# Two expert layers on one core: VectorE and GpSimd in written order, token operands on GpSimd, and a quarter of the weights converted a layer later

## The chip, the cores and the metric

The kernel is one launch on one core of a Trainium2 chip. The time is that of the device, in microseconds, and lower is better. Five engines work side by side, each through its own queue in order: TensorE (PE in the profile; PEld is its weight load), VectorE (DVE), ScalarE (ACT), GpSimd (POOL) and SyncE (SP), which here only issues DMAs.

## The reference, cut to what matters

```python
X = np.fft.rfft(x, axis=1)                       # x: 2 x 3008 x 256
Yr, Yi = ...                                     # X @ (w_r + i w_i) + bias, soft-shrunk by 0.01
y = np.fft.irfft(Y, n=3008, axis=1)              # 6016 tokens of 256
h = y @ w_in;  g = h * np.cos(h);  x = g @ w_out             # layer 1: 256 -> 2048 -> 256
h = x @ w_in2; g = h * np.clip(h + 3, 0, 6) / 6; x = g @ w_out2   # layer 2, the same shapes
```

The expert weights come as 64-bit floats. The kernel turns them into 32-bit floats itself, with integer operations on their bits ("conversion" below).

## The kernel before

Three parts follow each other: the Fourier part, expert layer 1 and expert layer 2. Every product of an expert layer keeps 32-bit precision by splitting each operand into a rounded high part and the rest (low part) and adding three matmuls: high by high, high by low, low by high (`three`).

An expert layer has six stages of 1024 tokens (the last 896), each as two halves of 512 (448). A stage (`jj`) has eight steps (`STEPS`), so the two layers have 96 steps `k`; a step is step `q = k % 8` of its stage. In a step, seven products of sums of the four quarter matrices (a Strassen form) make four blocks of h in four PSUM banks, called ha, hb, hc, hd: 21 matmuls. The four blocks of the step before (`Block`: ba, bd, be, bc) then go through w_out into `acc`: 24 matmuls. PE's order over the step is ha, (acc), hc, hb, ha, acc, hb, hd, acc, hb, acc.

Around it, each step has this work:
- ACT copies ha into hb (line 874) and hc into p5 (line 883). DVE then adds: `add(d, p5, b)` makes hd and `add(c, p5, b)` makes hc (line 764). PE can write hb again only when DVE has read it, so PE's next hb matmul waits for each add.
- For each block, `first` (ACT, then DVE) and, in layer 1 only, `second` (ACT Sin, DVE multiply, line 737) make g in the tile `r`; `split` rounds it to `gh` on ACT (line 743) and subtracts to get `gl` on POOL (line 744, through the helper at line 159).
- `operands(jj + 1)` makes the next stage's token operands `tok` out of the staged tokens `st`: four differences in place (`st<-st`) and seven subtractions for low parts (`tok<-st,tok`). Here DVE does them (line 399), but for four low parts in layer 1, which POOL does. It is a generator; `advance` takes one of its five pieces at a time, from the fifth step of a stage on. ACT writes the high parts.
- The `Converter` turns weights from 64 to 32 bits in chunks (kind "i" for w_in, "o" for w_out; layer m, quarter c, half k): a magnitude on ACT, five operations on DVE (clamp, shift, top, exponent, rest: lines 189 to 201), an addition on POOL (line 162), for "i" four sums on POOL, then the split into high and low parts (`pieces`, ACT line 260 and POOL). `other` asks for one conversion step at two places of a step, three in the first half of a stage, where one more is taken at the end. Quarters 0 and 3 of layer 1 are split directly into their tiles in SBUF; all others go to DRAM and are loaded later (`load_wi`, `load_wo`). All of layer 2's weights are converted during layer 1.
- In the first 13 steps, `y_mm` and `y_out` also finish the last rows of the inverse transform (yp, yo).

The order on PE, ACT and SP is the order of the program text (`manual_schedule`). On DVE and POOL a scheduler at build time decides the order.

Of the kernel before, what the change touches and what calls it, by code (L numbers as in the profile page):

```python
# [122 lines left out]
def fourier_moe_moe_kernel(ctx, tc, x, w_r, w_i, b_r, b_i, ta, tg, fg, win1, wout1, win2, wout2, out):  # L123
# [42 lines left out]
    def convert(kind, m, c, k):  # L166
# [54 lines left out]
        def pieces():  # L221
            direct = m == 0 and c in (0, 3)
# [10 lines left out]
            def tile(z):  # L233
                return persist.tile([128, 2, 256], F32R, tag="whi", bufs=3, name=f"whi{name}{z}")
# [31 lines left out]
    class Converter:  # L266


        def __init__(self):
            self.queue, self.loaded = [], []  # L270
            self.finished = set()
            self.prev, self.begun = None, False
            self.course = iter(())

        def add(self, m):
            for c in range(4):
                self.queue += [("i", m, c, 0), ("i", m, c, 1), ("o", m, c, 0), ("o", m, c, 1)]
            while len(self.loaded) < 2:
                self.load()
# [14 lines left out]
        def chunk(self):  # L294
            tail = self.tail()
            if self.loaded:
                key, ops = self.loaded.pop(0)
                if not self.begun:
# [12 lines left out]
                if ops["split"]:  # L311
                    self.prev = (key, ops)
                self.load()
            else:
                yield from tail
# [67 lines left out]
    def operands(jj):  # L383
# [25 lines left out]
        halve(B22, st[:, 1, 1])  # L409
        sub(st[:, 0, 0], st[:, 0, 1], st[:, 0, 0])  # L410
        yield
        sub(st[:, 0, 1], st[:, 1, 1], st[:, 0, 1])
        sub(st[:, 1, 1], st[:, 1, 1], st[:, 0, 0])
        act.activation(at(hi, T1, 2), st[:, 0], AF.Copy)
        yield
        sub(st[:, 1, 0], st[:, 1, 0], st[:, 1, 1])
        halve(T1, st[:, 0, 0])
        halve(T3, st[:, 0, 1])
        act.activation(at(hi, T4, 2), st[:, 1], AF.Copy)
        yield  # L420
        halve(T4, st[:, 1, 0])
        halve(T2, st[:, 1, 1])


    with ExitStack() as actx:
        apool = actx.enter_context(tc.tile_pool(name="apool", bufs=1))
        with tc.manual_schedule(engines={mybir.EngineType.PE, mybir.EngineType.SP, mybir.EngineType.Activation}):
# [83 lines left out]
            def late_loads3():  # L511
                cv.add(0)
# [76 lines left out]
            def shrink_hi(b, p):  # L589
                sh = persist.tile([128, 2, D], F32R, tag="gh", bufs=5, name=f"sh{b}_{p}")  # L590
# [91 lines left out]
            for i in range(NB * NP):  # L682
# [15 lines left out]
                elif i > 19:  # L698
                    next(ready, None)
            next(ready, None)  # L700
# [6 lines left out]
    with tc.manual_schedule(engines={mybir.EngineType.PE, mybir.EngineType.SP, mybir.EngineType.Activation}):  # L707
# [4 lines left out]
        class Block:  # L712
# [65 lines left out]
        def finish(jj, t):  # L778
            m, p = divmod(jj, NJ)
            n = HALF[p]  # L780
            for d, a in enumerate(acc.pop((jj, t))):
                o = persist.tile([128, 512], F32, tag="o", bufs=3, name=f"o{jj}_{t}{d}")
                if m == 0:
                    act.activation(o[:, :n], a[:, :n], AF.Copy)
                    sp.dma_start(x_dram[1][p][d, :, t * n : (t + 1) * n], o[:, :n])
                else:
                    act.activation(o[:, :n], a[:, :n], AF.Copy, scale=1.0 / 6.0)
# [10 lines left out]
        def w_loads(k):  # L798

            if k < 4:  # L800
                c = k // 2 + 1
                if k % 2 == 0:
                    load_wi(0, c)
                else:
                    load_wo(0, 2 * c)
                    load_wo(0, 2 * c + 1)
            elif k in (4, 5):
                cv.require(("i", 0, 3, 1) if k == 4 else ("o", 0, 3, 1))
            q = k - (G - STEPS)
            if 0 <= q < STEPS + 2 and q % 2 == 1:  # L810
                if q < STEPS:
                    load_wi(1, q // 2)
                if q > 2:
                    load_wo(1, q - 3)
                    load_wo(1, q - 2)
# [3 lines left out]
        def prepare(k):  # L819
# [4 lines left out]
            if q == 3:  # L824
# [3 lines left out]
        def advance(k):  # L828
            if k % STEPS > 3:
                next(ready, None)  # L830

        def other():
# [3 lines left out]
            if not pend:  # L836
                cv.step(1)
# [13 lines left out]
        cv.add(1)  # L851
# [10 lines left out]
        for k in range(2 * G):  # L862
# [16 lines left out]
            flush()  # L879
# [7 lines left out]
            add(d, p5, b, n)  # L887
            mm(a, A12, B21)
            prepare(k)
            advance(k)  # L890
            ba.first()
            flush()
# [3 lines left out]
            if k % STEPS < 4:  # L896
                other()
# [4 lines left out]
            other()  # L902
            bd.first()
            bc.first()
            out_next()
            y_begin()
            bd.second()
            y_end()
# [3 lines left out]
            advance(k)  # L912
# [3 lines left out]
            other()  # L916
            ba.split()
            old = bd, be, bc
            waiting += [ba, bd, be, bc]
            if k > 0 and k % STEPS < 4:  # L920
                cv.step(1)
# [51 lines left out]
```

## Time and profile before

| | before |
|---|---|
| median of 3 runs | 1261.34 us (1260.5 to 1261.72) |
| the profiled execution's own time | 1256.72 us |
| its span, first to last instruction | 1254.6 us |
| mean granted TensorE clock | 0.986 |
| PE busy | 1182.9 us (94%), 5377 matmuls |
| DVE busy | 814.6 us (65%), 1163 |
| ACT busy | 834.3 us (67%), 1530 |
| POOL busy | 680.8 us (54%), 536 |

The profile is of one execution. A group names the line, the engine and what is written from what. PE is busy nearly everywhere, so the shares say little; what counts is how long a step takes, and what PE waits for in a step that takes longer than another of its kind.

### The profile page before, as it was taken

Reading aid. Unit: us, or ns where it says so; the run is one execution under the profiler, and the core shown is the slowest. Engines: PE = TensorE matmul, PEld = TensorE weight load, DVE = VectorE, ACT = ScalarE, POOL = GpSimd, SP = SyncE. Lnnn points to the kernel's source line nnn. Section 1 sums busy time; section 2 is a strip of 40 time slices with the busy share of each in tenths; the row PEclk is TensorE's granted clock in tenths of the full one; section 3 lists DMA queues with packets and bytes.
Section 4 is the critical chain, followed back from the end, with each engine's and each line's share of the span. In section 5 each row is a group of like instructions: output and inputs, shape, how many; then the busy total and the mean of one; then the engine's idle time right before and its main releaser. Section 6 shows DMA issues by size and latency. Waiting matters only on the chain.

```text
span 1254.6 us, 15895 instructions
## 1 busy us (share of the span) xinstructions
PE 1182.9 (94%) x5377; PEld 975.7 (78%) x5379; DVE 814.6 (65%) x1163; ACT 834.3 (67%) x1530; POOL 680.8 (54%) x536
## 2 busy tenths in 40 slices
PE   8999979899988898989999999999999999999998
PEld 7888757687777676767778988788788887887897
DVE  4979695865586796896786684643744636436342
ACT  4677557677677777867777876556665566556654
POOL 0566335665466667676655554554545554555554
PEclk9999999999899899999999999999999999999999
DMA  9655837535410401320200435001010010010000
GB/s 249 186 153 147 268 96 223 182 96 161 158 66 17 160 34 43 118 85 34 102 21 1 179 132 189 1 1 68 1 60 8 1 68 1 1 63 1 34 1 30
DMA packets 51514, 107.75 MB, mean 86 GB/s; under 512 B 6404, under 2 KB 24328, under 8 KB 50664
## 3 DMA queue, kind: packets, MB, share of 16 engines
q1 hardware_dynamic: 51432, 106.74, 26.4%
q8 instruction: 42, 0.69, 0.2%
q14 instruction: 40, 0.33, 0.1%
HBM read 64.64 MB, written 42.07 MB: 85 GB/s over the span
## 4 chain that ended last, share of the span: by engine, by line
PE 65%; DVE 16%; ACT 6%; DMA 4%; issue 4%; POOL 3%; SPq 1%; POOLq 0%; ACTq 0%; DVEq 0%
PE acc L752 30%; PE hb L752 12%; PE ha L752 7%; PE hc L752 4%; PE hd L752 4%; DVE tok L399 3%; PE pp L537 3%; PE yp L355 2%; DVE r L737 2%; DVE r L728 2%; PE bp L564 2%; POOL gl L159 1%; DVE hc L764 1%; ACT gh L743 1%; PE zp L464 1%
## 5 line engine op out<-in xcount | busy, mean ns | idle before, releaser
L159 POOL TENSOR_TENSOR gl<-r,gh 128x512 fp32r<-128x512 f32 (+1 forms) x384 | 504.7, 1320 | 403.5 <-ACT gh L743 327.0
L752 PE MATMUL acc<-gh,wo 128*128 128x512 f32 (+1 forms) x1536 | 534.2, 389 | 0.0
L752 PEld LDWEIGHTS acc<-gh,wo 128*128 128x128 f32 x1536 | 291.3, 190 | 54.8
L752 PE MATMUL acc<-gl,wo 128*128 128x512 f32 (+1 forms) x768 | 299.3, 390 | 7.4 <-POOL gl L159 7.3
L752 PE MATMUL hb<-tok,wi 128*128 128x512 f32 (+1 forms) x864 | 247.8, 395 | 33.2 <-DVE hd L764 20.2
L743 ACT ACTIVATE gh<-r 128x512 fp32r<-128x512 f32 (+1 forms) x384 | 236.2, 616 | 9.8 <-DVE r L737 9.7
L752 PEld LDWEIGHTS hb<-tok,wi 128*128 128x128 f32 x864 | 160.4, 190 | 74.6 <-DVE hd L764 25.7
L752 PEld LDWEIGHTS acc<-gl,wo 128*128 128x128 f32 x768 | 145.7, 190 | 38.9 <-POOL gl L159 11.8
L752 PE MATMUL ha<-tok,wi 128*128 128x512 f32 (+1 forms) x576 | 160.6, 387 | 2.0 <-DMA wi<-wi_dram 1.2
L764 DVE TENSOR_TENSOR hd<-p,hb 128x512 f32<-128x512 f32 (+1 forms) x96 | 65.5, 683 | 144.7 <-PE hb L752 134.3
L736 ACT ACTIVATE r<-r 128x512 f32<-128x512 f32 (+1 forms) x192 | 118.8, 619 | 49.8 <-DVE r L728 49.4
L752 PEld LDWEIGHTS ha<-tok,wi 128*128 128x128 f32 x576 | 108.1, 188 | 23.3 <-ACT wi L260 1.6
L874 ACT ACTIVATE hb<-ha 128x512 f32<-128x512 f32 (+1 forms) x96 | 55.1, 574 | 52.0 <-PE ha L752 51.9
L883 ACT ACTIVATE p<-hc 128x512 f32<-128x512 f32 (+1 forms) x96 | 56.5, 589 | 49.8 <-PE hc L752 49.5
L764 DVE TENSOR_TENSOR hc<-p,hb 128x512 f32<-128x512 f32 (+1 forms) x96 | 65.3, 681 | 34.8 <-PE hb L752 34.6
L752 PE MATMUL hc<-tok,wi 128*128 128x512 f32 (+1 forms) x288 | 80.6, 388 | 5.3 <-DVE r L737 5.2
L752 PE MATMUL hd<-tok,wi 128*128 128x512 f32 (+1 forms) x288 | 82.4, 395 | 0.0
L737 DVE TENSOR_TENSOR r<-r,hb 128x512 f32<-128x512 f32 (+1 forms) x48 | 32.3, 673 | 63.3 <-ACT r L736 63.3
L730 ACT ACTIVATE r<-hd 128x512 f32<-128x512 f32 (+1 forms) x48 | 28.3, 589 | 62.4 <-PE hd L752 62.4
L752 PEld LDWEIGHTS hc<-tok,wi 128*128 128x128 f32 x288 | 53.5, 188 | 17.9 <-DVE r L737 8.2
L399 DVE TENSOR_TENSOR tok<-st,tok 128x512 fp32r<-128x512 f32 (+1 forms) x60 | 61.9, 1039 | 4.6 <-ACT tok L404 2.3
L752 PEld LDWEIGHTS hd<-tok,wi 128*128 128x128 f32 x288 | 55.7, 193 | 11.0
(140 smaller groups left out, 1684.3 us busy)
## 6 DMA issues: line engine op xcount, KB each, us to landing
wi<-wi_dram SPq DMA_DIRECT2D x6, 1792.0 KB, 7.5
st<-x_dram SPq DMA_DIRECT2D x20, 512.0 KB, 6.7
rawi<-in_win_dram SPq DMA_DIRECT2D x16, 512.0 KB, 4.6
rawo<-in_wout_dram SPq DMA_DIRECT2D x16, 512.0 KB, 3.9
u_dram<-v SPq DMA_DIRECT2D x48, 128.0 KB, 2.4
u_sb<-u_dram SPq DMA_DIRECT2D x16, 384.0 KB, 4.0
wo<-wo_dram SPq DMA_DIRECT2D x12, 512.0 KB, 8.2
x_dram<-o SPq DMA_DIRECT2D x20, 256.0 KB, 2.2
```

The costliest lines, as they stand in the source:

```text
L159: nc.gpsimd.tensor_tensor(out, x, y, op=ALU.subtract)
L355: pe.matmul(yp[:, i * TP : (i + 1) * TP], lhsT=u_sb[g][:, i, ec * 128 : (ec + 1) * 128], rhs=tg_sb[g][:, i * TP : (i + 1) * TP], start=Tru ...
L399: dve.tensor_tensor(out, x, y, op=ALU.subtract)
L537: pe.matmul(pp.rearrange("p a e -> p (a e)"), lhsT=za[:, p, kc, 2 * (k2 % 2) : 2 * (k2 % 2) + 2, :].rearrange("p r n -> p (r n)"), rhs=wb[ ...
L730: act.activation(r, h, AF.Relu, bias=3.0, scale=1.0)
L736: act.activation(r, r, AF.Sin, bias=math.pi / 2, scale=1.0)
L737: dve.tensor_tensor(r, r, self.h[:, : self.n], op=ALU.mult)
L743: act.activation(gh[:, :n], self.r[:, :n], AF.Copy)
L752: pe.matmul(h[:, :n], lhsT=w, rhs=x, start=start and j == 0, stop=stop and j == 2, skip_group_check=True)
L764: dve.tensor_tensor(h[:, :n], r[:, :n], x[:, :n], op=ALU.add)
L874: act.activation(b[:, :n], a[:, :n], AF.Copy)
L883: act.activation(p5[:, :n], c[:, :n], AF.Copy)
```

## The change

In the expert layers DVE and POOL join the engines that keep the order of the text. The token operands' eleven subtractions go to POOL, one at a time in twelve pieces (DVE keeps them for one stage, `jj == NJ + 1`, prepared in layer 2's first stage), and begin two steps earlier. The conversion is asked for less often, once or twice in a step, in most of layer 1. Layer 2's quarter 3 is no longer converted in layer 1: it is loaded at the end of it and converted in layer 2's first steps, directly into its tiles; layer 1's quarter 3 goes through DRAM instead. Half of the copies out of `acc` move from ACT to DVE. The tile ring `gh` has 4 buffers in place of 5, and `whi` 4 in place of 3.

```diff
-            direct = m == 0 and c in (0, 3)
+            direct = (m, c) in ((0, 0), (1, 3))
...
-                return persist.tile([128, 2, 256], F32R, tag="whi", bufs=3, name=f"whi{name}{z}")
+                return persist.tile([128, 2, 256], F32R, tag="whi", bufs=4, name=f"whi{name}{z}")
...
                 if not self.begun:
+                    for _ in range(3):
+                        next(tail, None)
+                        yield
                     ops["magnitude"]()
                 for part in ("clamp", "shift", "top", "exponent", "rest"):
                     ops[part]()
-                    next(tail, None)
+                    if part != "clamp":
+                        next(tail, None)
...
-        def sub(out, x, y):
-            dve.tensor_tensor(out, x, y, op=ALU.subtract)
-
-        def halve(t, src):
-            (pool_sub if jj < NJ and t >= T1 else sub)(at(lo, t), src, f32(at(hi, t)))
-
-        act.activation(at(hi, B11), st[:, 0, 0], AF.Copy)
-        act.activation(at(hi, B21, 2), st[:, 1], AF.Copy)
-        halve(B11, st[:, 0, 0])
-        halve(B21, st[:, 1, 0])
+        subtract = (dve if jj == NJ + 1 else nc.gpsimd).tensor_tensor
+
+        def high(t, src):
+            act.activation(at(hi, t), src, AF.Copy)
+
+        def low(t, src):
+            subtract(at(lo, t), src, f32(at(hi, t)), op=ALU.subtract)
+
+        def less(z, x, y):
+            subtract(z, x, y, op=ALU.subtract)
+
+        b11, b12, b21, b22 = (st[:, e, t] for e in range(2) for t in range(2))
+        high(B11, b11)
+        high(B21, b21)
         yield
...
+        less(b11, b12, b11)
+        yield
+        less(b12, b22, b12)
+        high(T1, b11)
+        yield
...
-                sh = persist.tile([128, 2, D], F32R, tag="gh", bufs=5, name=f"sh{b}_{p}")
+                sh = persist.tile([128, 2, D], F32R, tag="gh", bufs=4, name=f"sh{b}_{p}")
...
-                    next(ready, None)
-            next(ready, None)
+                    for _ in range(3):
+                        next(ready, None)
+            for _ in ready:
+                pass
...
-    with tc.manual_schedule(engines={mybir.EngineType.PE, mybir.EngineType.SP, mybir.EngineType.Activation}):
+    engines = {mybir.EngineType.PE, mybir.EngineType.SP, mybir.EngineType.Activation, mybir.EngineType.DVE, mybir.EngineType.Pool}
+    with tc.manual_schedule(engines=engines):
...
-                gh = persist.tile([128, 512], F32R, tag="gh", bufs=5, name=f"gh{self.tag}")
+                gh = persist.tile([128, 512], F32R, tag="gh", bufs=4, name=f"gh{self.tag}")
...
-                    act.activation(o[:, :n], a[:, :n], AF.Copy)
+                    if d == 0:
+                        act.activation(o[:, :n], a[:, :n], AF.Copy)
+                    else:
+                        dve.tensor_copy(o[:, :n], a[:, :n])
...
-            if k < 4:
-                c = k // 2 + 1
-                if k % 2 == 0:
-                    load_wi(0, c)
-                else:
-                    load_wo(0, 2 * c)
-                    load_wo(0, 2 * c + 1)
-            elif k in (4, 5):
-                cv.require(("i", 0, 3, 1) if k == 4 else ("o", 0, 3, 1))
+            if k in (0, 2, 4):
+                load_wi(0, k // 2 + 1)
+            elif k in (1, 3, 6):
+                load_wo(0, 2 * (k // 2) + 2 - 2 * (k == 6))
+                load_wo(0, 2 * (k // 2) + 3 - 2 * (k == 6))
...
+            if k == G - 3:
+                cv.add(1, range(3, 4))
+            if k == G + 5:
+                cv.require(("i", 1, 3, 1))
+            elif k == G + 6:
+                cv.require(("o", 1, 3, 1))
...
-            if q == 3:
+            if q == (1 if jj else 3):
                 stage_in(jj + 1)
                 ready = operands(jj + 1)
 
-        def advance(k):
-            if k % STEPS > 3:
+        def advance(k, spare):
+            if k % STEPS > (1 if k >= STEPS else 3) and not (spare and k >= STEPS):
                 next(ready, None)
 
-        def other():
+        def other(k, place):
             nonlocal pend
             for f in pend[:2]:
                 f()
-            if not pend:
-                cv.step(1)
+            if not pend and (place == 0 or (place == 2 and k % 2) or k < STEPS or k >= G - 2):
+                cv.step(1 + (place == 2 and (k < 6 or k > G)))
             pend = pend[2:]
...
-        cv.add(1)
+        cv.add(1, range(3))
...
             mm(a, A12, B21)
             prepare(k)
-            advance(k)
+            advance(k, False)
             ba.first()
-            flush()
             out_next()
             if old:
                 oe.split()
-            if k % STEPS < 4:
-                other()
+            other(k, 0)
             ba.second()
             mm(b, S3, T3)
             add(c, p5, b, n)
             mm(d, S4, B22)
-            other()
+            other(k, 1)
             bd.first()
+            advance(k, True)
             bc.first()
```

PE's order stays as it is, matmul for matmul. On DVE this is the place between the end of step 17 and the middle of step 18 (layer 1, third stage) before the change; r17_10 is the block be of step 17, hd_18 and hc_18 are the two adds, and cva and cvb are tiles of the conversion.

```order
L737 TENSOR_TENSOR r17_11_3906<-r17_11_3906,hc_17_3821 128x512
L189 TENSOR_SCALAR cvao111_3518<-cvao111_3518 128x512
L192 TENSOR_SCALAR cvao111_3518<-cvao111_3518 128x512
L195 SCALAR_TENSOR_TENSOR cvao111_3518<-rawo111_3517,cvao111_3518 128x512
L198 TENSOR_SCALAR cvbo111_3519<-cvao111_3518 128x512
L201 SCALAR_TENSOR_TENSOR cvbo111_3519<-rawo111_3517,cvbo111_3519 128x512
L737 TENSOR_TENSOR r17_10_3922<-r17_10_3922,hb_17_3820 128x512
L764 TENSOR_TENSOR hd_18_3956<-p5_18_3976,hb_18_3954 128x512
L728 SCALAR_TENSOR_TENSOR r18_00_3989<-r18_00_3989,ha_18_3953 128x512
L764 TENSOR_TENSOR hc_18_3955<-p5_18_3976,hb_18_3954 128x512
```

The same place on DVE with the change:

```order
L762 TENSOR_TENSOR r17_11_3890<-r17_11_3890,hc_17_3816 128x512
L195 SCALAR_TENSOR_TENSOR cvai110_3469<-rawi110_3468,cvai110_3469 128x512
L762 TENSOR_TENSOR r17_10_3906<-r17_10_3906,hb_17_3815 128x512
L789 TENSOR_TENSOR hd_18_3926<-p5_18_3946,hb_18_3924 128x512
L753 SCALAR_TENSOR_TENSOR r18_00_3962<-r18_00_3962,ha_18_3923 128x512
L198 TENSOR_SCALAR cvbi110_3470<-cvai110_3469 128x512
L762 TENSOR_TENSOR r18_00_3962<-r18_00_3962,ha_18_3923 128x512
L789 TENSOR_TENSOR hc_18_3925<-p5_18_3946,hb_18_3924 128x512
```

Five conversion operations of one chunk stood in a row ahead of the add into hd; now one stands there, the next comes behind the add, and the multiply of block ba (r18_00) comes ahead of the add into hc.

On POOL this is step 27 (layer 1, fourth stage) before the change, from block bd of step 26 to block ba of step 27:

```order
L159 TENSOR_TENSOR gl26_01_4907<-r26_01_4856,gh26_01_4906 128x512
L162 TENSOR_TENSOR w32_13_4992<-cvai130_4604,cvbi130_4605 128x512
L159 TENSOR_TENSOR w32_13_4992<-w32_13_4992 128x256
L159 TENSOR_TENSOR gl26_11_4924<-r26_11_4859,gh26_11_4923 128x512
L159 TENSOR_TENSOR gl26_10_4947<-r26_10_4873,gh26_10_4946 128x512
L159 TENSOR_TENSOR gl27_00_4996<-r27_00_4937,gh27_00_4995 128x512
```

The same step on POOL with the change, one of those with the most work (tok4 are the next stage's operands, w32_11 and cvao110 are of the conversion):

```order
L159 TENSOR_TENSOR gl26_01_4825<-r26_01_4782,gh26_01_4824 128x512
L159 TENSOR_TENSOR gl26_11_4842<-r26_11_4785,gh26_11_4841 128x512
L410 TENSOR_TENSOR tok4_4751<-st4_4647,tok4_4751 128x512
L159 TENSOR_TENSOR gl26_10_4863<-r26_10_4799,gh26_10_4862 128x512
L162 TENSOR_TENSOR cvao110_4114<-cvao110_4114,cvbo110_4115 128x512
L159 TENSOR_TENSOR w32_11_4072<-w32_11_4072,whii111h4_4771 128x512
L159 TENSOR_TENSOR w32_11_4072<-w32_11_4072,whii111h6_4871 128x256
L410 TENSOR_TENSOR tok4_4751<-st4_4647,tok4_4751 128x512
L159 TENSOR_TENSOR gl27_00_4923<-r27_00_4853,gh27_00_4922 128x512
```

An operand subtraction now stands ahead of the last gl of step 26, and three conversion operations and a second operand subtraction ahead of the first gl of step 27.

## Rows read from the trace of the kernel before

**Rows 1.** Windows: busy us (x instructions) of PE, PEld, DVE, ACT, POOL; clock; DMA.

```profile
0.00:174.20 174.20, 162.27 (x835) 135.14 (x838) 134.95 (x202) 109.14 (x206) 72.75 (x63) 0.98 0.66 190
...
174.20:755.80 581.60, 529.93 (x2354) 430.57 (x2354) 431.62 (x618) 430.67 (x792) 353.85 (x278) 0.98 0.30 100
755.80:1250.20 494.40, 490.68 (x2191) 409.98 (x2189) 248.04 (x346) 294.00 (x533) 254.23 (x196) 1.00 0.09 32
...
920.50:1003.10 82.60, 82.13 (x361) 67.38 (x360) 43.77 (x60) 49.56 (x88) 42.70 (x32) 1.00 0.07 26
```

**Rows 2.** Windows of single undisturbed steps: 512 columns, with yp, 448 columns.

```profile
615.83:626.03 10.20, 10.20 (x46) 8.45 (x45) 6.50 (x11) 8.20 (x16) 6.43 (x5) 1.00 0.15 52
...
271.40:283.60 12.20, 12.20 (x63) 10.18 (x62) 8.43 (x12) 8.71 (x16) 8.60 (x9) 1.00 0.41 119
707.69:716.81 9.12, 9.12 (x46) 8.45 (x45) 5.96 (x11) 7.22 (x16) 4.62 (x4) 1.00 0.06 11
```

**Rows 3.** Waits of PE's weight loads in layer 1: total us, times, longest.

```profile
PEld hb L752 <- DVE hd L764: 25.7, 14, 3.8
...
PEld acc L752 <- POOL gl L159: 10.8, 10, 2.7
...
PEld hc L752 <- DVE r L737: 8.2, 7, 2.7
...
PEld hb L752 <- DVE hc L764: 6.6, 5, 2.7
...
PEld yp L355 <- DVE r L737: 6.5, 4, 3.2
PEld hb L752 <- ACT hb L874: 6.5, 4, 3.6
```

**Rows 4.** Timeline of step 18: start, us, engine, line, [idle before <- releaser].

```profile
418.38 0.42 DVE L189 TENSOR_SCALAR cvao<-cvao 128x512 f32<-128x512 f32 x1
...
424.85 0.70 DVE L764 TENSOR_TENSOR hd<-p,hb 128x512 f32<-128x512 f32 x1
...
425.60 1.65 PE L752 MATMUL hb<-tok,wi 128*128 128x512 f32 x3 [2.91 <-DVE hd L764]
```

**Rows 5.** Windows of PE's wait in step 18 and of what follows.

```profile
422.40:425.60 3.20, 0.29 (x3) 0.00 (x1) 3.03 (x5) 0.63 (x1) 2.11 (x3) 0.89 0.20 18
425.60:431.74 6.14, 6.14 (x15) 4.84 (x16) 3.79 (x6) 2.35 (x4) 2.34 (x2) 0.50 0.93 324
```

**Rows 6.** Timeline of step 34, undisturbed.

```profile
618.38 0.69 DVE L737 TENSOR_TENSOR r<-r,hb 128x512 f32<-128x512 f32 x1 [1.81 <-ACT r L736]
...
619.49 0.69 DVE L764 TENSOR_TENSOR hd<-p,hb 128x512 f32<-128x512 f32 x1 [0.42 <-ACT p L883]
...
620.06 2.66 POOL L159 TENSOR_TENSOR gl<-r,gh 128x512 fp32r<-128x512 f32 x2 [0.81 <-ACT gh L743]
...
620.80 0.69 DVE L728 SCALAR_TENSOR_TENSOR r<-r,ha 128x512 f32<-128x512 int32 x1 [0.62 <-ACT r L727]
...
621.27 0.84 PE L752 MATMUL hb<-tok,wi 128*128 128x512 f32 x3
621.71 0.62 ACT L736 ACTIVATE r<-r 128x512 f32<-128x512 f32 x1
...
623.99 0.84 PE L752 MATMUL hb<-tok,wi 128*128 128x512 f32 x3
...
624.90 0.39 PE L752 MATMUL acc<-gl,wo 128*128 128x512 f32 x1
```

**Rows 7.** Durations by line: ns min/median/max, first and last start.

```profile
L399 DVE TENSOR_TENSOR tok<-st,tok x60: 615/912/1786, 156.0 to 1149.7; 128x512 fp32r<-128x512 f32 x50, 128x448 fp32r<-128x448 f32 x10
...
L195 DVE SCALAR_TENSOR_TENSOR cvao<-rawo,cvao x16: 676/1661/1786, 42.9 to 604.1; 128x512 uint32<-128x512 uint32 x16
...
L159 POOL TENSOR_TENSOR gl<-r,gh x384: 1133/1291/1860, 189.4 to 1246.5; 128x512 fp32r<-128x512 f32 x160, 128x448 fp32r<-128x448 f32 x32
```

**Rows 8.** DMA issues of the page: KB each, median us to landing.

```profile
wo<-wo_dram SPq DMA_DIRECT2D x12, 512.0 KB, 8.2
```

More of the change, by code (lines that the diff above doesn't have):

```diff
@@ L271, in __init__, with add @@
             self.finished = set()
-            self.prev, self.begun = None, False
+            self.prev, self.begun, self.busy = None, False, 0
             self.course = iter(())
-        def add(self, m):
-            for c in range(4):
+        def add(self, m, cs):
+            for c in cs:
                 self.queue += [("i", m, c, 0), ("i", m, c, 1), ("o", m, c, 0), ("o", m, c, 1)]
-            while len(self.loaded) < 2:
+            while len(self.loaded) < 2 - self.busy and self.queue:
                 self.load()
@@ L297, in chunk @@
                 key, ops = self.loaded.pop(0)
+                self.busy = 1
                 if not self.begun:
+                    for _ in range(3):
+                        next(tail, None)
+                        yield
                     ops["magnitude"]()
@@ L312, in chunk @@
                     self.prev = (key, ops)
+                self.busy = 0
                 self.load()
@@ L396, in at @@
             return z[:, t - s0] if count == 1 else z[:, t - s0 : t - s0 + count]
-        def sub(out, x, y):
-            dve.tensor_tensor(out, x, y, op=ALU.subtract)
-        def halve(t, src):
-            (pool_sub if jj < NJ and t >= T1 else sub)(at(lo, t), src, f32(at(hi, t)))
-        act.activation(at(hi, B11), st[:, 0, 0], AF.Copy)
-        act.activation(at(hi, B21, 2), st[:, 1], AF.Copy)
-        halve(B11, st[:, 0, 0])
-        halve(B21, st[:, 1, 0])
+        subtract = (dve if jj == NJ + 1 else nc.gpsimd).tensor_tensor
[8 more added lines that the diff above has]
+        high(B21, b21)
         yield
-        halve(B22, st[:, 1, 1])
-        sub(st[:, 0, 0], st[:, 0, 1], st[:, 0, 0])
+        low(B11, b11)
+        high(B22, b22)
         yield
-        sub(st[:, 0, 1], st[:, 1, 1], st[:, 0, 1])
-        sub(st[:, 1, 1], st[:, 1, 1], st[:, 0, 0])
-        act.activation(at(hi, T1, 2), st[:, 0], AF.Copy)
+        low(B21, b21)
         yield
[L416 to L419, printed above, removed]
+        low(B22, b22)
         yield
-        halve(T4, st[:, 1, 0])
-        halve(T2, st[:, 1, 1])
+        less(b11, b12, b11)
[3 more added lines that the diff above has]
+        yield
+        less(b22, b22, b11)
+        high(T3, b12)
+        yield
+        less(b21, b21, b22)
+        high(T2, b22)
+        yield
+        low(T1, b11)
+        high(T4, b21)
+        yield
+        low(T3, b12)
+        yield
+        low(T2, b22)
+        yield
+        low(T4, b21)
     with ExitStack() as actx:
@@ L511, in late_loads3 @@
             def late_loads3():
-                cv.add(0)
+                cv.add(0, range(4))
             def constants(k):
@@ L798, in w_loads @@
         def w_loads(k):
[L800 to L815 removed]
+            if k in (0, 2, 4):
[3 more added lines that the diff above has]
+                load_wo(0, 2 * (k // 2) + 3 - 2 * (k == 6))
+            q = k - (G - STEPS)
+            if q in (1, 3, 5):
+                load_wi(1, q // 2)
+            if q in (3, 5, 7):
+                load_wo(1, q - 3)
+                load_wo(1, q - 2)
+            if k == G - 3:
[4 more added lines that the diff above has]
+                cv.require(("o", 1, 3, 1))
         ready = iter(())
@@ L911, in fourier_moe_moe_kernel @@
             be.first()
-            advance(k)
+            advance(k, False)
             bc.second()
@@ L915, in fourier_moe_moe_kernel @@
             out_next()
-            other()
+            other(k, 2)
             ba.split()
+            flush()
             old = bd, be, bc
             waiting += [ba, bd, be, bc]
-            if k > 0 and k % STEPS < 4:
-                cv.step(1)
             w_loads(k)
```

9 lines of the change are left out of this document (6 added, 3 removed).

## The prediction

> **What bounds the kernel now.** I began with the windows by part, since the shares of the page cannot tell a full PE from one that waits a little in every step. The Fourier part takes 174.2 us, layer 1 581.6, layer 2 494.4 up to its last step's end, for the same matmuls in either layer [rows 1]. Next I looked for steps that nothing disturbs. With 512 columns such a step takes 10.20 us (45 matmuls, so 0.227 us each), with 448 columns 9.12, and a step that also carries the yp matmuls 12.20 [rows 2]. So layer 1 without any wait would be 40 x 10.20 + 8 x 9.12 + 13 x 2.0 = 507 us: 75 of its 581.6 us are lost. Layer 2 loses little: its stages take 82.6 us against 81.6 [rows 1].
>
> The waits of PE's weight loads say to whom the 75 us go [rows 3]. Four rows name DVE: 25.7 + 8.2 + 6.6 + 6.5 = 47 us. POOL's gl has 10.8, ACT's copy into hb 6.5. The rest is the clock: layer 1 was granted 0.98 of it [rows 1], and 2% of 581.6 us is 12. The sum, 76, closes.
>
> The timeline of step 18 shows what a DVE wait is. From 418.38 DVE works through five conversion operations and the multiply for block be, and only at 424.85 begins the add into hd; PE has waited 2.91 us for it when its hb matmul starts at 425.60 [rows 4]. All that time DVE was busy (3.03 of 3.20 us): it did the wrong thing first. After the wait the granted clock is 0.50, the level of 1.2 GHz, for 6.14 us, and 15 matmuls take that long where 15 x 0.227 = 3.4 us would do [rows 5]. So a wait of 2.9 us costs 5.6.
>
> **The change, part by part.** *DVE in written order.* The text never has more than one conversion operation between two operations of a block in layer 1's later steps, so I ask what one costs at each of its two places. Ahead of the multiply for be, DVE was idle for 1.81 us anyway in the undisturbed step [rows 6], and the longest such operation takes 1.79 [rows 7]: free. Ahead of the multiply for ba there is less room. DVE ends the operation before at 620.80 + 0.69 = 621.49, and the Sin for which the multiply waits ends at 621.71 + 0.62 = 622.33: 0.84 us of idle time. Then come the multiply (0.69) and the add into hc (0.69), which would end at 623.71, while PE wants hb at 623.99: 0.28 more [rows 6]. An operation of up to 1.1 us is free there, one of 1.79 makes PE wait 0.7. The L195 operation takes between 0.68 and 1.79 us, at the median 1.66 [rows 7], so it costs some 0.5. The cheapest operation is free; hence 0 to 0.7 us for each of some 35 operations at this place, 0 to 25 us. I take 7: two of the five operations of a chunk at 0.5 us. DVE's term falls from 47 to 7.
>
> Why the same operation takes 0.68 or 1.79 us is a matter of POOL running beside it; the operands' subtractions with both inputs in SBUF spread the same way, from 0.62 to 1.79 [rows 7]. The Trainium skill, "SBUF — State Buffer", section "Who interferes with whom", says that a DVE instruction with two SBUF inputs and a GpSimd instruction that reads SBUF take turns at a shared port, each holding it for its whole length. By that rule POOL's longer hours would put more of the conversion at the upper end: the 25 us above in place of my 7.
>
> *The operands on POOL.* By the two orders 97 subtractions leave DVE, each of about 0.9 us, the median of those into tok [rows 7]; 46 of them are layer 1's, over 40 us of DVE's 431.6 [rows 1]. POOL gets them at about the 1.29 us of a gl [rows 7]: 46 x 1.29 = 59 us on top of its 353.9, less one converted quarter of 14 instructions (some 16 us). That makes near 400 of 530 us, 75%. What matters is the order: an operand subtraction now stands ahead of the last gl of each block set. In the undisturbed step that gl ends at 620.06 + 2.66 = 622.72 and PE uses it at 624.90 [rows 6]; after a subtraction of 1.29 us 0.9 are left. Where three conversion operations come as well (step 27 in the listing), POOL has nine operations of about 1.2 us, 11 in 10.2, and is a little late. POOL's row of 10.8 us stays about as it is: I take 9, with bounds of 3 (only bursts) and 25 (0.5 us in each of 50 steps).
>
> *ACT.* It gives half of the copies out of acc to DVE, which puts them behind the add into hd and has idle time there, and writes the high parts singly instead of in pairs. Its load in layer 1 falls from 430.7 us [rows 1] by about 10 us, a converted quarter's splits and copies. I keep 5 of its 6.5 us of waits, within 3 and 15.
>
> *The clock.* With no block of DVE work longer than 1.8 us, waits of about 3 us like that of step 18 should be gone, and with them the low clock: from 12 to 2, within 0 and 8.
>
> *Quarter 3.* The conversions of one quarter leave layer 1 and enter layer 2's first stage, and a stage of layer 2 has DVE busy for 43.8 of 82.6 us and POOL for 42.7 [rows 1]. Twenty DVE operations of at most 1.79 us, and 14 POOL operations of at most 1.86 [rows 7], fit. The DMAs balance: layer 1's quarter 3 now writes 12 pieces to DRAM and is loaded from there, layer 2's no longer is. On SP these loads stand behind the step's yo stores, and one pair is issued only at the end of step 6, to be used about 4 us into step 7; such a load takes 8.2 us at the median [rows 8]. It costs 0 to 4 us, I take 2. In layer 2 the 1.0 us of each stage goes away for the four stages prepared on POOL, and the first stage gets 2 us longer (0 to 8): net -2, within -5 and +6.
>
> *The Fourier part* has its first operands on POOL too. PE is idle for 12 of 174.2 us there and POOL has 100 us free [rows 1]; I take -2, within -6 and +3.
>
> *The tile rings.* `gh` with 4 buffers is just enough: a block's gh is written one step after the block four before it, whose matmuls are over by then in written order. The work that hides it is PE's own step; if PE is late, ACT waits with it, and the cost is in ACT's bound.
>
> **The sum.** Layer 1 loses 7 + 9 + 5 + 2 + 2 = 25 us in place of 75: -50. Layer 2 -2, Fourier part -2. Against the profiled execution's own 1256.7 us (span 1254.6) this gives 1202.7. The median of the runs was 1261.3, 4.6 above, so I forecast 1207. The upper bounds in layer 1 (25 + 25 + 15 + 8 + 4 = 77) would eat the whole gain, the lower ones (0 + 3 + 3) leave only 6 us lost, -69 and with the other parts -80.
>
> **The rivals.** *POOL becomes the bound (slower).* In some 50 steps POOL must take two operand subtractions besides four gl. If the conversion and the contention (a gl takes up to 1.86 us, not 1.29 [rows 7]) use up the 0.9 us that are left, the last gl of each such step comes late by a whole subtraction, 50 x 1.29 = 65 us, and the time is 1207 + 65 = 1272. It decides from 54 / 50 = 1.1 us per step on. For it: POOL is in strict order now, and in step 27 it has more than 10.2 us to do. Against it: 75% mean load, and few steps like that one. The Trainium skill, "GPSIMD Engine Reference", section "Engine selection", sends two-input elementwise work to VectorE because GpSimd needs about twice as long. The trace agrees on the ratio: a gl takes 1.29 us, the multiply for be 0.69 [rows 6, 7]. Chance 9%.
>
> *ACT takes DVE's place (half the gain).* An undisturbed step has ACT busy for 8.2 of 10.2 us with one conversion operation [rows 2]; steps with highs of operands, copies out of acc and two conversion operations have two or three more of 0.6 us, close to 10. If every second step of layer 1's 48 lost 1 us to that, the time would be 1231. Against it: ACT's waits total only 6.5 us now [rows 3]. Chance 20%.
>
> *The order does not matter (no change).* DVE's waits might come from its load rather than its order: 431.6 of 581.6 us [rows 1]. But the moved operands take over 40 us from that load anyway. 1259 to 1264, chance 3%.
>
> **Numbers.** My forecast, 1190 to 1222, gets 60%; ACT, 1222 to 1250, 20%; better than 1190 (the lower bounds) 8%; no change 3%; slower 9%. Two runs of this kernel differ by about 0.1%, so 0.2% is about what can be told from no change. Faster is 60 + 20 + 8 = 88%. The range 1187 to 1242 holds the first, three quarters of the second and half of the third: 80%.
>
> **What would show it.** Right: in layer 1 the waits of hb on DVE's adds shrink to under 15 us, the granted clock reads 1.00 in nearly every stage, stages take 82 to 86 us after the first two, DVE has no row of subtractions at the operands' lines outside one stage. Wrong: PE waiting for gl in most steps with operand work (the slower rival); ACT's copies into hb or p5 at the head of the waits; layer 2's first stage above 90 us; or a wait for wo in step 7 beyond 4 us.

## The result, and the profile after

| | before | after |
|---|---|---|
| median, 4 runs each | 1260.92 us (1260.21 to 1261.72) | 1206.14 us (1202.39 to 1207.45) |
| ratio | | 0.9561, interval 0.9538 to 0.9583 |
| the profiled execution's own time, span | 1256.72, 1254.6 us | 1207.45, 1205.6 us |
| mean granted TensorE clock | 0.986 | 0.987 |
| DVE, POOL busy | 814.6, 680.8 us | 739.9, 794.9 us |

The windows by part after (busy us of PE, PEld, DVE, ACT, POOL; clock; DMA): the Fourier part, layer 1, layer 2, then layer 1's first, third and sixth stage and layer 2's first and third.

```profile
0.00:174.80 174.80, 162.64 (x836) 135.69 (x838) 125.11 (x188) 110.15 (x209) 82.50 (x70) 0.97 0.66 186
174.80:710.30 535.50, 521.58 (x2353) 428.41 (x2352) 380.67 (x568) 419.93 (x790) 391.51 (x309) 0.98 0.35 115
710.30:1200.80 490.50, 489.18 (x2191) 410.42 (x2190) 233.46 (x335) 292.97 (x545) 320.88 (x254) 1.00 0.08 26
...
174.80:287.00 112.20, 103.01 (x473) 82.88 (x472) 71.09 (x109) 78.23 (x148) 68.14 (x53) 0.92 0.61 205
...
380.10:464.10 84.00, 83.48 (x362) 66.98 (x361) 65.13 (x94) 67.94 (x127) 63.50 (x49) 1.00 0.16 51
...
629.90:710.30 80.40, 77.18 (x361) 68.48 (x360) 56.82 (x92) 63.78 (x130) 62.15 (x51) 0.98 0.53 184
...
710.30:793.30 83.00, 82.39 (x361) 67.16 (x361) 65.61 (x83) 54.84 (x102) 60.97 (x46) 1.00 0.11 37
...
874.90:956.50 81.60, 81.60 (x361) 67.59 (x360) 33.70 (x51) 48.65 (x90) 54.87 (x43) 1.00 0.07 26
```

Against [rows 1], layer 1 gives 46.1 of the 49.0 us by which the span fell and layer 2 3.9; the Fourier part is 0.6 longer. By stages, layer 1 took 109.4, 109.5, 100.7, 97.3, 88.4 and 76.3 us and now takes 112.2, 93.1, 84.0, 83.5, 82.3 and 80.4. So the gain is made in stages two to five; in these two executions the first and the last became longer.

PE's busy time in the windows parts layer 1's loss. Before, PE stood idle for 581.60 - 529.93 = 51.7 us, and it was busy 22.9 us longer than the 507 of undisturbed steps. Now it is idle for 535.50 - 521.58 = 13.9 and busy 14.6 too long. Both together: 74.6 before, 28.5 now.

The waits of PE's weight loads in layer 1 after answer to [rows 3]:

```profile
PEld hb L777 <- DVE hc L789: 10.7, 23, 1.1
PEld acc L777 <- POOL gl L159: 4.0, 3, 2.5
PEld acc L777 <- DMA wo<-wo_dram: 3.9, 1, 3.9
PEld yp L361 <- ACT yo L371: 3.5, 12, 0.4
PEld ha L777 <- ACT yo L371: 2.6, 5, 0.9
PEld yp L361 <- DVE r L762: 2.4, 2, 1.9
PEld ha L777 <- ACT gh L768: 1.7, 1, 1.7
PEld bp L586 <- DVE ph L573: 1.4, 1, 1.4
PEld hb L777 <- DVE hd L789: 0.6, 1, 0.6
```

The row that was first, the add into hd, fell from 25.7 us to 0.6. The add into hc now leads, but as 23 short waits of at most 1.1 us. A weight load can wait while the matmul ahead of it still runs, so these rows overstate. PE's own idle time, after, in the same window:

```profile
PE acc L777 <- DMA wo<-wo_dram: 3.5, 1, 3.5
PE acc L777 <- POOL gl L159: 3.0, 2, 2.1
PE hb L777 <- DVE hc L789: 2.2, 9, 0.7
PE yp L361 <- DVE r L762: 1.5, 1, 1.5
```

Step 18 after, the place of [rows 4], in the timeline:

```profile
401.73 1.58 DVE L195 SCALAR_TENSOR_TENSOR cvai<-rawi,cvai 128x512 uint32<-128x512 uint32 x1
...
404.49 0.70 DVE L789 TENSOR_TENSOR hd<-p,hb 128x512 f32<-128x512 f32 x1 [0.42 <-PE hb L777]
...
407.04 0.42 DVE L198 TENSOR_SCALAR cvbi<-cvai 128x512 uint32<-128x512 uint32 x1
...
407.82 0.69 DVE L762 TENSOR_TENSOR r<-r,ha 128x512 f32<-128x512 f32 x1 [0.37 <-ACT r L761]
408.43 0.69 DVE L789 TENSOR_TENSOR hc<-p,hb 128x512 f32<-128x512 f32 x1
409.17 0.96 PE L777 MATMUL hb<-tok,wi 128*128 128x512 f32 x3
```

One conversion operation stands ahead of the add into hd, which now waits for PE and not PE for it. The multiply for ba and the add into hc follow each other without a gap, and PE's hb matmul starts as soon as hc is read.

Three places still lose more: step 7 (17.69 us instead of 12.2), step 42 (13.08, before 9.12), and steps 0 and 1 (17.08 and 14.71, before 14.57 and 13.23). The timelines of PE and POOL at the three, in order of time:

```profile
174.00 0.49 PE L586 MATMUL bp<-ph,fgr 128*128 128x512 f32 x1 [1.31 <-ACT ph L572]
...
176.19 2.50 PE L586 MATMUL bp<-ph,fgr 128*128 128x512 f32 x5 [0.86 <-DVE ph L573]
...
277.23 0.76 PE L777 MATMUL acc<-gh,wo 128*128 128x512 f32 x1 [3.51 <-DMA wo<-wo_dram]
...
651.69 1.30 POOL L162 TENSOR_TENSOR cvao<-cvao,cvbo 128x512 f32<-128x512 f32 x1 [4.03 <-DVE cvbo L201]
652.94 1.98 POOL L159 TENSOR_TENSOR w<-w,whii121h 128x512 fp32r<-128x512 f32 x2
654.88 3.33 POOL L159 TENSOR_TENSOR gl<-r,gh 128x448 fp32r<-128x448 f32 x3
...
656.05 0.65 PE L777 MATMUL acc<-gl,wo 128*128 128x448 f32 x1 [2.09 <-POOL gl L159]
```

and the windows that follow the last wait of each, with the whole of step 0 behind them:

```profile
176.19:181.48 5.29, 5.29 (x13) 4.13 (x13) 1.23 (x2) 2.10 (x4) 0.00 (x0) 0.50 0.28 104
...
277.23:280.75 3.52, 3.52 (x8) 2.77 (x9) 0.00 (x1) 0.00 (x0) 3.01 (x3) 0.52 0.00 0
...
656.05:660.00 3.95, 3.94 (x12) 3.56 (x13) 3.03 (x4) 1.57 (x3) 3.95 (x4) 0.57 0.99 309
...
174.80:191.88 17.08, 14.01 (x50) 10.33 (x48) 9.57 (x16) 8.81 (x17) 0.00 (x0) 0.70 0.32 89
```

Ahead of step 0 and in it PE waits for parts of a Fourier product (`ph`), in step 7 for w_out of quarter 3 (the pair of loads issued at the end of step 6). In step 42 POOL, now in strict order, stood for 4.03 us at the addition of a conversion, which needed DVE's last operation of that chunk. Two more conversion operations and three gl were queued behind it, and PE waited 2.09 us for the first gl. After each of these waits the clock was half or little more.

Durations by line after (ns min/median/max) answer to [rows 7]:

```profile
L410 POOL TENSOR_TENSOR tok<-st,tok x77: 1154/1299/1791, 155.5 to 1117.2; 128x512 fp32r<-128x512 f32 x63, 128x448 fp32r<-128x448 f32 x14
...
L195 DVE SCALAR_TENSOR_TENSOR cvao<-rawo,cvao x16: 675/1046/1797, 48.0 to 765.3; 128x512 uint32<-128x512 uint32 x16
```

### The profile page after: what moved, and what is told of

Read it like the earlier page. It is cut to its first block, busy times and chain, and to the rows that moved or that the text cites. A ratio compares the mean times of both kernels' runs of the same rounds, so it can differ in the third digit from the quotient of the medians.

```text
span 1205.6 us, 15893 instructions
## 1 busy us (share of the span) xinstructions
PE 1173.4 (97%) x5377; PEld 974.5 (81%) x5379; DVE 739.9 (61%) x1090; ACT 823.1 (68%) x1542; POOL 794.9 (66%) x633
## 5 line engine op out<-in xcount | busy, mean ns | idle before, releaser
L777 PEld LDWEIGHTS hb<-tok,wi 128*128 128x128 f32 x864 | 160.4, 190 | 41.7 <-DVE hc L789 12.2
L410 POOL TENSOR_TENSOR tok<-st,tok 128x512 fp32r<-128x512 f32 (+1 forms) x77 | 100.0, 1301 | 2.2 <-ACT tok L407 2.2
L162 POOL TENSOR_TENSOR w<-cvai,cvbi 128x512 f32<-128x512 f32 x16 | 20.9, 1308 | 73.4 <-DVE cvbi L201 73.4
L777 PEld LDWEIGHTS hc<-tok,wi 128*128 128x128 f32 x288 | 54.9, 191 | 10.5
```

What stands on the lines that cost most here:

```text
L162: nc.gpsimd.tensor_tensor(out, x, y, op=ALU.add)
L410: subtract(at(lo, t), src, f32(at(hi, t)), op=ALU.subtract)
L777: pe.matmul(h[:, :n], lhsT=w, rhs=x, start=start and j == 0, stop=stop and j == 2, skip_group_check=True)
```

## The experiments

The theory was that the written order on DVE makes the gain: no block of conversion ahead of an add. The rival was that load makes it: 97 subtractions leave DVE, and the conversion is asked for less often. All edits are of the changed kernel; ratios are to the kernel before, with their 95% intervals. The tile rings, the copies out of `acc` on DVE and the new places at which work is asked for stay in all of them; none of these was taken back by itself.

| | DVE | POOL | operands | conversion | median us | ratio |
|---|---|---|---|---|---|---|
| the change | written | written | POOL | new | 1206.14 | 0.9561 [0.9538, 0.9583] |
| `e2_no_order` | scheduled | scheduled | POOL | new | 1254.42 | 0.9951 [0.9933, 0.9968] |
| `e3_dve_order` | written | scheduled | POOL | new | 1242.53 | 0.9861 [0.9837, 0.9884] |
| `e4_pool_order` | scheduled | written | POOL | new | 1218.67 | 0.9673 [0.9632, 0.9714] |
| `e1_order_alone` | written | written | as before | new | 1210.83 | 0.9604 [0.9578, 0.9631] |
| `e5_quarter3_back` | written | written | POOL | old | 1219.69 | 0.9681 [0.9654, 0.9708] |
| `e9_order_only` | written | written | as before | old | 1227.58 | 0.9740 [0.9706, 0.9774] |
| `e10_conversion_only` | scheduled | scheduled | as before | new | 1232.44 | 0.9786 [0.9743, 0.9829] |

**Which order counts.** Three kernels take engines out of the written order:

```diff
-    engines = {... Activation, mybir.EngineType.DVE, mybir.EngineType.Pool}
+    engines = {... Activation}                            # e2_no_order
+    engines = {... Activation, mybir.EngineType.DVE}      # e3_dve_order
+    engines = {... Activation, mybir.EngineType.Pool}     # e4_pool_order
```

> The change with the order on DVE and POOL left to the scheduler, all else as in the change, operands on POOL too. Theory 'order': blocks of conversion operations come ahead of the adds again, waits of 2 to 3 us with half clock behind them return, 1230 to 1255. Rival 'load': DVE has lost its subtractions, so 1205 to 1212.

> The change with DVE in written order and POOL's order left to the scheduler. Theory 'order': it is DVE's order that counts, 1203 to 1215. If POOL's order counts as much: 1225 or more.

> The change with POOL in written order and DVE's order left to the scheduler. Theory 'order' on DVE: the waits of hb on DVE's adds return, 1225 to 1250. If POOL's order is what counts: 1205 to 1212.

Without any order nearly the whole gain is gone, so the lighter load that this kernel leaves on DVE does not make it. But the theory's stress on DVE fell: DVE's order alone brings 12 us (1254.4 to 1242.5), POOL's alone 36 (to 1218.7). Taken away from the change, DVE's order costs 12.5 us and POOL's 36.4. The result of `e4_pool_order` lies between the two ranges that were expected. In the kernel with DVE's order alone the waits of PE's weight loads in layer 1 show gl where before stood the add:

```profile
PEld acc L777 <- POOL gl L159: 18.7, 11, 3.7
PEld hb L777 <- DVE hc L789: 9.7, 17, 1.0
```

and its timeline of step 34 why:

```profile
589.26 2.45 POOL L410 TENSOR_TENSOR tok<-st,tok 128x448 fp32r<-128x448 f32 x2
591.67 2.35 POOL L413 TENSOR_TENSOR st<-st 128x448 f32<-128x448 f32 x2
593.97 1.26 POOL L159 TENSOR_TENSOR gl<-r,gh 128x512 fp32r<-128x512 f32 x1
595.29 0.50 PE L777 MATMUL acc<-gl,wo 128*128 128x512 f32 x1 [3.25 <-POOL gl L159]
```

The scheduler lets four operand subtractions run in a row ahead of a gl, whatever PE needs. It does so in the third step of most stages, in layer 2 too, whose later stages take 84.5 to 85.9 us in the kernel without any order, where the change takes 81.6. That is what DVE's block of conversion was before, on the other engine. With POOL's order alone the block on DVE is back: 20.9 us of weight loads wait for the add into hd in layer 1, 12 times.

**Order and operands.** `e1_order_alone` gives the operands' subtractions back to DVE (four low parts to POOL), as before:

```diff
-            subtract(at(lo, t), src, f32(at(hi, t)), op=ALU.subtract)
+            (nc.gpsimd if jj < NJ and t >= T1 else dve).tensor_tensor(at(lo, t), src, f32(at(hi, t)), op=ALU.subtract)
...
-            subtract(z, x, y, op=ALU.subtract)
+            dve.tensor_tensor(z, x, y, op=ALU.subtract)
```

> The change, but the token operands' subtractions on DVE and POOL as they were shared before (all on DVE but four low parts in layer 1), now in written order. Theory 'order' (the gain is that no block of conversion work stands ahead of an add): layer 1 keeps most of its gain, 545 to 555 us in place of the change's 535.5, the DVE adds wait a little more, total 1212 to 1225. Rival 'load' (the gain is the 46 subtractions that leave DVE in layer 1): layer 1 stays above 565 us, total 1235 or more.

So 50 of the 55 us come without that move. The add into hc is waited for longer (19.2 us of weight loads, now 10.7), and layer 1's stages two to six take 429.7 us where the change takes 423.3. The stretch ahead of them is shorter: from layer 1's first matmul to step 2 it takes 28.7 us where the change's takes 32.3. In all the medians differ by some 5 us, with intervals that just overlap, and the total is a little under the range that was expected.

**Quarter 3 and the rate.** `e5_quarter3_back` converts all of layer 2's weights in layer 1 again, at the old rate and with the old places of loads. `e9_order_only` joins this to the edit of `e1_order_alone`; `e10_conversion_only` keeps the new conversion and takes the operands' edit and the scheduled order.

```diff
-            direct = (m, c) in ((0, 0), (1, 3))
+            direct = m == 0 and c in (0, 3)
...
-            if not pend and (place == 0 or (place == 2 and k % 2) or k < STEPS or k >= G - 2):
-                cv.step(1 + (place == 2 and (k < 6 or k > G)))
+            if not pend and (place or k % STEPS < 4):
+                cv.step(1 + (place == 2 and k > 0 and k % STEPS < 4))
...
-        cv.add(1, range(3))
+        cv.add(1, range(4))
```

> The change with all of layer 2's weights converted in layer 1 again, at the old rate (four conversion steps in a step of a stage's first half, two in the second) and with the old loads; DVE and POOL in written order. Theory 'order': single operations between block operations still cost 0 to 0.7 us each, so with two to four in a step layer 1 loses some 10 to 20 us more and layer 2's first stage is some 1 to 1.5 us shorter, total 1212 to 1225. Rival (the conversion's amount in layer 1 is what had to go): 1235 or more. If it is free: 1206.

> Written order on DVE and POOL, but both other parts undone: the operands' subtractions shared as before (e1), and all of layer 2's weights converted in layer 1 at the old rate (e5). It is the order nearly alone. If the parts add up as in e1 (4.7 us) and e5 (13.5 us) against the change's 1206: 1222 to 1227. If DVE, which then has both loads, is the bound: 1235 or more. If order is worth little without the other parts: 1250 or more.

> The order on DVE and POOL left to the scheduler and the operands' subtractions shared as before; the conversion's new rate and the last quarter in layer 2 stay. It is the conversion nearly alone. If order is what counts: 1240 to 1258, with waits of hb on DVE's adds of 2 to 3 us. If the lower rate of conversion is enough to keep DVE's blocks short: 1215 to 1225.

By ratio times 1260.9, the written order is worth 33 us with the old conversion (before to e9, with the rings, copies and places that no kernel takes back) and 23 with the new one (e10 to e1). The thinner conversion is worth 27 without the order (before to e10, with the same additions) and 17 to 15 with it. The two overlap; that both keep DVE's conversion away from the adds would explain it. The operands' move costs 21 us in scheduled order (e10 to e2) and gains 7 (e9 to e5) or 5 (e1 to the change) in written order, where the intervals of either pair just overlap. The result of `e10_conversion_only` lies between its two expected ranges. What either engine's order is worth by itself was tried only with the operands on POOL. `e10_conversion_only` still has 25.7 us of weight loads waiting for the add into hd, in 16 waits, as much as the kernel before [rows 3]. The text before the change, put in written order as it was, was not tried: also in e9 the places at which work is asked for are the new ones.

**What still waits.** Three kernels mend or worsen one wait each: of each pair of w_out loads (steps 1, 3 and 6) the second is needed first, so `e6_first_needed_first` swaps them; `e7_conversion_behind_add` asks for the first conversion operation behind the add into hc, except where work left over from the Fourier part (`pend`) is still queued; `e8_all_on_pool` leaves no stage's operands on DVE.

```diff
-                load_wo(0, 2 * (k // 2) + 2 - 2 * (k == 6))   # e6: behind the next line
                 load_wo(0, 2 * (k // 2) + 3 - 2 * (k == 6))
+                load_wo(0, 2 * (k // 2) + 2 - 2 * (k == 6))
...
-            other(k, 0)                                       # e7: if not pend, behind add(c, p5, b, n)
...
-        subtract = (dve if jj == NJ + 1 else nc.gpsimd).tensor_tensor
+        subtract = nc.gpsimd.tensor_tensor                    # e8
```

> The change with the two loads of each pair of w_out tiles issued the other way round, so that the one that is used first is loaded first. The wait of acc for a DMA in step 7 of the change is 3.5 us, followed by some 3.5 us at half clock. If the second load of a pair lands some 2 us behind the first: the wait falls to 1 to 2 us, total 2 to 4 us less than the change. If both land together: no difference.

> The change with the first conversion step of a step placed behind the add into hc, in place of between the two operations of block ba. Theory (the conversion operation at that place is what delays the add): the 12.2 us in which PE's weight loads wait for the add into hc fall below 3 us, total 4 to 8 us less than the change. Rival (the add waits for ACT's Sin or for its own turn anyway, or the operation now delays the next block's part and a later wait takes its place): no difference within 2 us.

> The change with the operands of the one stage that DVE keeps on POOL as well, so that POOL has them together with the conversion of the last quarter in layer 2's first stage. If POOL has room (75 to 80% busy): that stage stays at 83 us, total within 2 us of the change. If POOL is the bound when both meet, as the slower rival of the prediction had it: waits of acc for gl of 1 to 2 us in three or four steps, the stage 86 to 90 us, total 1209 to 1214.

With the swap step 7 takes 14.51 us instead of 17.69, the total is 1202.43 us, 0.9537 [0.9519, 0.9554]. PE's wait for w_out fell from 3.5 to 1.9 us; the rest is the clock, which stays at 1.00 behind it. That part need not be the swap's: `e7_conversion_behind_add`, without it, waits 3.04 us for the same load, keeps the full clock behind it, and has step 7 at 15.64 us:

```profile
278.39:281.91 3.52, 3.52 (x15) 2.93 (x16) 1.15 (x2) 0.41 (x1) 3.05 (x3) 1.00 0.00 0
```

With the conversion behind the add the total is 1202.00, 0.9533 [0.9519, 0.9547]. Both intervals overlap the change's. The waits of e7's weight loads in layer 1:

```profile
PEld acc L777 <- POOL gl L159: 6.2, 6, 2.6
...
PEld hb L777 <- DVE hc L789: 3.8, 6, 1.8
```

The wait for hc fell by 7 us, that for gl rose by 2, and layer 1 fell by 4.7, to 530.8. Its stages two to six took 418.6 us, against 423.3 in the change and 423.1 in `e8_all_on_pool`, which has the change's work there. So the conversion operation ahead of ba's multiply does cost what the prediction looked for there: some 4.5 us, where the prediction took 7 within 0 and 25. With all operands on POOL the total is 1208.07, 0.9585 [0.9560, 0.9609], not told from the change. Its first stage of layer 2 takes 87.0 us instead of 83.0, which is what the exception saves there:

```profile
704.90:791.90 87.00, 83.00 (x362) 66.96 (x360) 56.62 (x73) 55.01 (x101) 71.70 (x57) 1.00 0.10 35
```

**Both, and the joint.** `e11_both` has the edits of e6 and e7; `e12_both_and_first_operands` also shares the first stage's operands, made in the Fourier part, between DVE and POOL as before:

```diff
-        subtract = (dve if jj == NJ + 1 else nc.gpsimd).tensor_tensor
+        subtract = (dve if jj in (0, NJ + 1) else nc.gpsimd).tensor_tensor
...
-            subtract(at(lo, t), src, f32(at(hi, t)), op=ALU.subtract)
+            (nc.gpsimd.tensor_tensor if jj == 0 and t >= T1 else subtract)(at(lo, t), src, f32(at(hi, t)), op=ALU.subtract)
```

> The change with the edits of e6 and e7 together. If their gains add (3.7 and 4.1 us): 1197 to 1200. If the wait of one takes the gain of the other: 1201 to 1203.

> e11 with the operands of the first stage, which the Fourier part prepares, shared between DVE and POOL as before the change. In e1, which had that, the Fourier part and the first two steps took 197.3 us, in the change and in e6 and e7 206: if the cause is this, 3 to 8 us less than e11 there and 1190 to 1196 in all. If those first steps only vary from run to run (e8, with the change's own order there, took 201): no difference beyond 2 us.

Together e6 and e7 give 1202.39, 0.9545 [0.9514, 0.9577], no more than either. In its trace the later stages are those of e7, but step 7 is at 17.14 us in spite of the swap, and steps 0 and 1 at 17.08 and 15.10. With the first operands shared the total is 1196.84, 0.9509 [0.9468, 0.9549], the lowest of all, with an interval that overlaps that of e11. Step 0 in its trace:

```profile
173.70:185.35 11.65, 9.17 (x41) 6.64 (x39) 6.80 (x11) 7.99 (x16) 0.00 (x0) 0.90 0.25 63
```

This is not the change's step 0 made shorter. In the four kernels here that share these operands with DVE (e1, e9, e10, e12) eight matmuls of the Fourier part stand ahead of layer 1's first ha matmul, while in the change and in the kernel before they stand behind it: the window has 41 matmuls, the change's 50. From layer 1's first matmul (of hb) to step 2 the work is the same everywhere, 108 matmuls. The four take 28.3 to 31.1 us for it, the nine with these operands on POOL 27.3 to 32.6, the kernel before 28.3. So the traces don't show that the shared operands shorten the joint; the change and e8, with the same work there, differ by 3.6 us (32.3 and 28.7). The cause of e12's lower total stays open.

## Why the prediction was right, point by point

**The total** was forecast at 1207 and came at 1206.1. The parts are less exact than that: the sum of -54 stands against -49.3 between the profiled executions and -54.8 between the medians. The execution profiled after was the longest of its four, the one before lay 4.2 us under its median. That the total came within 1 us is luck in part, since the terms below missed in both directions. The prediction took two runs of a kernel to differ by 0.1%; the four of the change spread over 0.4%.

**Layer 1** (-50, measured -46.1): the mechanism was right as far as it goes: the long waits behind DVE's blocks are gone, stages three to five take 82 to 84 us, and the clock reads 1.00 in stages two to five. But the prediction put 40 of the 50 us under "DVE in written order", and DVE's order by itself is worth 12.5 us of the change (e4). The thinner conversion takes its share, 15 to 17 us, and POOL's written order, which the prediction named only as a risk, is worth 36: without it two thirds of the gain are gone (e3).

- *DVE*, 47 to 7, measured 10.7 + 2.4 + 0.6 = 13.7 by the same weight-load rows: mis-sized, twice the term, though most is hidden under running matmuls (3.9 us of PE's idle time). e7 puts the price of the conversion ahead of ba's multiply at 7 us of such waits.
- *POOL*, 9 with bounds 3 and 25, measured 4.0. Here the trace's one long wait (step 42) isn't an operand subtraction ahead of a gl, as I costed it, but POOL's queue standing at a conversion's addition that waits for DVE. I named no work queued behind that wait.
- *ACT*, 5: the row that this term was made of, the copies into hb, fell from 6.5 to 0.3. What ACT is waited for now is 3.5 + 2.6 + 1.7 = 7.8, mostly for yo. That was so before as well (5.8 us), in rows that the sum left out:

```profile
PEld yp L355 <- ACT yo L365: 4.4, 12, 1.0
PEld yp L355 <- DVE cvai L192: 2.3, 1, 2.3
PEld ha L752 <- ACT wi L260: 1.6, 1, 1.6
PEld ha L752 <- ACT yo L365: 1.4, 2, 0.7
PEld hb L752 <- POOL tok L159: 0.8, 1, 0.8
```

- *The load of w_out*, 2 with bounds 0 and 4: 3.9, the upper bound, and the half clock behind it, for which the term had nothing. Step 7 lost 5.5 us.
- *The clock*, 12 to 2: the step that failed, above its upper bound of 8. By the same reading, 8% of the first stage's 112.2 us (clock 0.92) and 2% of the last's 80.4 (0.98) make 10.6 now. I expected the low clock behind DVE's blocks alone; it follows the waits at the three places above too, and two of them lie in the first stage. Nor did my account of before close as its sum of 76 has it: the rows just shown are 10.5 us more, and PE's idle time was 52 us, not the 64 of the weight-load rows I added up, its busy time 23 too long, not 12. That the sum met the 75 was luck. The clock of 0.98 explains about half of that excess; in stages at 1.00 some 0.7 to 1.9 us of it remain, whose cause these rows don't show.

**Layer 2** (-2, measured -3.9): its later stages, 81.6, are undisturbed. The first takes 83.0, far from the 90 that would have been wrong; e8 shows that it would be 87.0 if its operands were not on DVE. **The Fourier part** (-2, measured +0.6) gained nothing, and in the profiled executions the joint behind it got worse.

**The rivals.** POOL as the bound: the prediction counted POOL's strict order for this rival, and the runs show the reverse. PE waits for gl in the third step of most stages where POOL is not in written order (e2 and e3), 36 us slower than e4 and the change. With the order PE waits for gl in layer 1 in step 42, 2.09 us, and in step 4, 0.88 us. The Trainium skill, "GPSIMD Engine Reference", section "Engine selection", sends two-input work to VectorE because GpSimd takes about twice as long. For the operands' subtractions the medians here are 1.30 us on POOL and 0.91 on DVE [rows 7], less than twice. Moving them cost 21 us in scheduled order; in written order it gained 5 to 7, with intervals that just overlap.

That ACT would take DVE's place was wrong: its waits, by all rows, fell from 13.9 us to 8.1. The prediction's argument against this rival, that ACT's waits total only 6.5 us, had left the rows of yo and wi out. That order does not matter fell with e2.

By the rule of the Trainium skill, "SBUF — State Buffer", section "Who interferes with whom", a busier POOL would have put more conversion operations at the upper end of their durations. The spread is still there, 675 to 1797 ns, but the median of L195 fell from 1661 [rows 7] to 1046, with POOL busy for 391.51 us of layer 1 instead of 353.85 [rows 1]. The cost of 25 us that I derived from it did not come. That POOL is what makes them long fits both traces: of the 32 L195 operations of either execution, those over 1.1 us, 20 before and 14 after, each ran beside a POOL operation. Of the short ones 11 of 12 before and 9 of 18 after ran with POOL idle.

## What to carry to other kernels

Take the loss of a stretch as PE's idle time plus the excess of its busy time over undisturbed steps; waits of weight loads tell who is late, but not how much it costs. Before moving work to an engine off the critical path, look at the order of that engine's queue: here the same move cost 21 us with a scheduler's order and gained some 5 us with an order by what PE needs next. With a strict order, look for the instruction in each queue that waits for another engine's leisurely work, and for what stands behind it.

## What was unexpected of the hardware

A wait of PE can cost about twice its length, when the granted clock falls behind it: 3.51 us in step 7 were followed by 3.52 us at 0.52, 2.09 us in step 42 by 3.95 us at 0.57. It doesn't take one long wait: at the start of layer 1 gaps of 0.51, 1.31 and 0.86 us within 5 us were followed by 5.29 us at 0.50, the level of 1.2 GHz. But the clock does not always fall. In `e2_no_order` PE waits 2.57 us for gl at the same place of two stages of layer 2, steps 66 and 74; here are the windows behind the two waits:

```profile
943.47:947.00 3.53, 3.53 (x9) 2.83 (x10) 0.69 (x1) 1.61 (x3) 2.36 (x2) 0.56 0.00 0
1029.40:1033.00 3.60, 3.60 (x16) 2.99 (x17) 0.69 (x1) 2.73 (x5) 2.43 (x2) 1.00 0.00 0
```

The first lets 9 matmuls through, the second 16. The wait of 3.04 us in step 7 of e7 left the clock at 1.00 as well. These traces don't show what decides it. So the prediction's 5.6 us for a wait of 2.9 are the price of that one wait, and not of each.
